# A spectral block on one core: the token table held in full for both halves, fewer filler products, and the special unit two groups later

## The chip, the cores and the metric

The kernel runs on one core of one Trainium2 chip. The metric is device time of one execution in microseconds. Three runs of the kernel as it was before the change gave 255.28 (median), 255.12 and 256.31. A difference of more than 0.5% (about 1.3 us) is about what a measurement of this kernel can tell from no change.

The core has five engines that run their own instruction streams in order: TensorE (PE: matmuls; its weight loads, PEld, overlap the matmuls), VectorE (DVE), ScalarE (ACT), GpSimd (POOL) and SyncE (SP, which issues most DMAs). They wait for one another with semaphores.

## The reference, cut to what matters

```
mod = (silu(c) @ w_mod).reshape(1, 6, 1, 640)      # sa, ca, ga, sb, cb, gb
h = layernorm(x) * (1 + ca) + sa                   # x: 2048 tokens x 640 channels
X = rfft2(h) * (w_r + 1j * w_i)                    # over tokens and channels
x = x + ga * irfft2(X)
h = layernorm(x) * (1 + cb) + sb
x = x + gb * ((silu(h @ w_gate) * (h @ w_up)) @ w_down)   # 640 -> 1728 -> 640
```

All inputs and the output are bf16.

## The kernel before, in words

The work runs in four stages, one after the other.

**The token stage** (lines 326 to 494) normalises x and takes both Fourier transforms as matmuls with tables. A token's number is 1024 h + 8 p + t, with half h = 0 or 1, partition p and residue t = 0 to 7. There is one pass for each residue t:

- `xpair`/`xhat` write the two normalised tiles of the pass (one per half). `rstd_of` takes a short step on VectorE and a power on GpSimd (line 344), then VectorE writes `nmean`, and GpSimd (line 356) or VectorE (line 354) applies them. For passes 4, 5 and 6 GpSimd does both tiles. The tiles lie in three buffers (`xhs`) in turn. The statistics (`bn`, lines 329 and 330) are VectorE's.
- `st_a(t)` (line 370) is ten matmuls. For each of five groups of 128 channels it multiplies half 0's tile and then half 1's tile by 256 columns of the token table `Mtab` (cosines and negative sines of 128 frequencies), and adds the two in PSUM. There is one PSUM area for it, `zA`.
- `ht_ev(t)` (line 373) copies `zA` to bf16 on ScalarE. In pass 7 VectorE copies the last part.
- `st_b(t, ck)` (lines 379 and 381), for ck = 0 and 1, transforms the channels with the tables `Rs`, and `a_ev(t, ck)` (line 385) copies the results into `A_sb`, on ScalarE but for three copies on VectorE and the split last pass.

TensorE's order is `st_a(0)`, then for t = 0 to 7: some filler products (`idle2`, line 362; dummy matmuls into a PSUM bank that nobody reads from there), `st_a(t+1)`, `st_b(t, 0)`, `st_b(t, 1)`. Because `zA` exists once, `st_a(t+1)` may start only when `ht_ev(t)` has read it.

Only half 0's part of the token table is loaded (`load_m`, line 258: 256 columns for each t into the right half of a 512-column row). Moving by 1024 tokens multiplies frequency k by (-1)^k, so half 1's table is half 0's with every second column negated. `m_odd` (line 262, ScalarE, three calls) writes those negated columns into the left half of the row, and half 1's matmuls read columns alternately from the left and the right half:

```
rhs = _rev(Mtab, 512 * t + 256 * (1 - h), [[2, 128], [257, 2]] if h else [[1, 256]])
```

The constants share SyncE's DMA queue with x, the spectral weights and the modulation weights. SyncE issues in program order, and a DMA also waits for the one issued eight before it. GpSimd issues two DMAs (line 282) that write flipped copies of the spectral weights to DRAM; SyncE loads these back later (line 474).

**The mixing stage** (lines 497 to 775) works on 81 channel frequencies l in 21 groups, g = 0 to 20. Each l is a 128x128 block of `A_sb`, which has to be transposed. The first 18 blocks are transposed by TensorE (`t2_pe`); the other 63 by four DMA transposes that SyncE issues as soon as `A_sb` is complete (`t2_dma`, line 509; l = 1 to 15, 16 to 31, 32 to 47, 64 to 79). `mix(g)` (line 547) reads the transposed blocks, `prod` (line 571, VectorE) multiplies by the spectral weights, `stage_b` (line 578) and `stage_c` (lines 600 and 603) transform back, with ScalarE copies (lines 581 and 612) between, into `Em` and `Er`. In the loop over g (line 738), step g does `mix(g+2)`, `prod(g+2)`, `stage_b(g)` and, at every second g, `stage_c`. The first step that reads a block from a DMA transpose is g = 3, with `mix(5)`. GpSimd forms sums of the spectral weights meanwhile (`wsum`, line 390).

**The special unit** is a side computation in this loop for the token frequencies that are multiples of 128; they take partition 127 of `Em` and `Er`. `sp_gather` (line 638, GpSimd) collects one column from all the transposed blocks, so it needs the last DMA transpose. `sp_mm` and `sp_ev` are three rounds of small matmuls and copies, at the steps g in `SPG = (8, 10, 12)`; round 0 (line 647) reads the gathered columns and stands ahead of `mix(g+2)` in TensorE's queue. Round 2 ends with two copies on ScalarE (line 674) and two DMAs that GpSimd issues (lines 675 and 676) into partition 127 of `Em` and `Er`. These have to land before `s1em(0)` (line 697), the first matmuls of the next stage.

**The last two stages** transform back over tokens and channels, add x (lines 1209 to 1266), and run the second layernorm and the feed-forward network (from line 1268), where TensorE is the bound.

The order of the work is written out by hand; no scheduler moves it.

Of the kernel before, what the change touches and what calls it, by code (L numbers as in the profile page):

```python
# [18 lines left out]
NT, P = 16, 128  # L19
# [8 lines left out]
_NPBF = ml_dtypes.bfloat16  # L28
# [59 lines left out]
def _tables():  # L88
    if _TABLE_CACHE:
        return _TABLE_CACHE  # L90
    T = {}
# [8 lines left out]
    p = np.arange(P, dtype=np.float64)  # L100
    kap = p + 1
    M = np.zeros((P, 8, 1, 2, 128))
    H = np.zeros((128, 8, 2, P))
    for t in range(8):
        a = 2.0 * np.pi * ((kap[None, :] * (8 * p[:, None] + t)) % S) / S
        for h in range(1):
            b = 2.0 * np.pi * ((kap[None, :] * (1024 * h + 8 * p[:, None] + t)) % S) / S
            M[:, t, h, 0], M[:, t, h, 1] = np.cos(b), -np.sin(b)
        M[:, t, :, 0, 127], M[:, t, :, 1, 127] = 1.0, ((-1.0) ** p)[:, None]
        H[:, t, 0], H[:, t, 1] = np.cos(a.T), np.sin(a.T)  # L110
        H[127, t, 0], H[127, t, 1] = 1.0, (-1.0) ** p
    T["M"] = M[:, :, 0].reshape(P, 8, 256).astype(_NPBF)
    T["H"] = H.astype(_NPBF)
# [47 lines left out]
def _rev(ap, free_off, dims):  # L161
    a = ap[:]
    return bass.AP(tensor=a.tensor, offset=a.offset + free_off, ap=[list(a.ap[0])] + [list(d) for d in dims])
# [3 lines left out]
def adaln_block_kernel(ctx, tc, A_x, A_w_r, A_w_i, B_x, B_w_gate, B_w_up, B_w_down, c, w_mod, out):  # L167
    nc = tc.nc
    T = _tables()
# [17 lines left out]
    rE = _Region(big, "rE", 40960, "E")  # L187
# [41 lines left out]
    RI = rH.cut(8192, [2, 4, 160])  # L229
    Mtab = rE.cut(0, [8, 512])  # L230
    Rs = rE.cut(8192, [2, 4, RC])
# [25 lines left out]
    def load_m(lo, hi):  # L257
        nc.sync.dma_start(Mtab[:, lo:hi, 256:512], M_dram[:, lo:hi])

    def m_odd(lo, hi):  # L260
        o = Mtab[:, lo:hi].rearrange("p t (b k two) -> p t b k two", b=2, two=2)[:, :, :, :, 0]
        nc.scalar.mul(o[:, :, 0], o[:, :, 1], -1.0)

# [62 lines left out]
    if True:  # L326
# [33 lines left out]
        def idle2(n):  # L360
            for i in range(n):
                nc.tensor.matmul(psum[:, 3, 256:512], lhsT=ones[:], rhs=ones[:].unsqueeze(1).to_broadcast([P, 2, 128]), start=True, stop=True)

        def st_a(t):
            xh = xhs[t % 3]
            for c5 in range(NC5):
                for h in range(2):
                    lhsT = xh[:, h, 512:640] if c5 == 4 else xh[:, h, 0:512].rearrange("p (m r) -> p r m", r=4)[:, c5, :]
                    rhs = _rev(Mtab, 512 * t + 256 * (1 - h), [[2, 128], [257, 2]] if h else [[1, 256]])
                    nc.tensor.matmul(zA[:, c5], lhsT=lhsT, rhs=rhs, start=(h == 0), stop=(h == 1))  # L370

# [41 lines left out]
        nc.scalar.activation(sc_f[:], cps, ACT.Silu)  # L413
        m_odd(0, 1)
        act_stats(3)
# [18 lines left out]
        st_a(0)  # L434
        m_odd(1, 3)
        ht_ev(0)
# [17 lines left out]
        for t in range(8):  # L454
            if t + 1 < 8:
                idle2(6 if t == 0 else 2)
                st_a(t + 1)
                ht_ev(t + 1, 0, 3 if t == 6 else NC5)
                if t == 6:
                    ht_ev(7, 3, 5, nc.vector.tensor_copy)  # L460
            if t == 0:
                m_odd(3, 8)
            u = 2 * t + 6
# [38 lines left out]
    if True:  # L502
# [208 lines left out]
        PPs, Y2s = {}, {}  # L711
        SPG = (8, 10, 12)
        t2_pe(0)
# [24 lines left out]
        for g in range(NG + 1):  # L738
            for lo, rk in {1: ((16, 0), (16, 8)), 4: ((32, 0), (32, 8)), 8: ((64, 0), (64, 8))}.get(g, ()):
                wsum(lo, lo + 16, rk, nc.gpsimd)  # L740
            if g == 3:
                sp_w(1)
            if g == 5:
                nc.gpsimd.tensor_copy(sgnc[:], Kstab[:, 576:577])
            if g == 6:
                sp_gather()
# [620 lines left out]
```

## Time and profile before

| | us |
|---|---|
| three runs | 255.28 median (255.12 to 256.31) |
| the profiled execution | 256.88 |
| its span, from the first to the last instruction | 255.1 |
| busy in the span: TensorE | 245.1 (96%) |
| VectorE | 204.9 (80%) |
| ScalarE | 168.5 (66%) |
| GpSimd | 72.4 (28%) |

The profiled execution took 1.78 us more than its span, and 1.60 us more than the median of the three runs. In the trace the token stage lasts until about 38.6 us of the span, the mixing stage until about 70 us, the stage after it until about 90 us. PE in the profile counts filler products as busy too. "L370" is line 370; "x10" is ten instructions, and the time beside them is that of the group. What stands in square brackets is the engine's idle time before, and who ended it. In the table of windows the columns are the window, its length, the busy time (and number of instructions) of each engine, the granted TensorE clock, the busy share of the DMA engines, and what they moved.

### The profile page before, as it was taken

Reading aid. Unit: us, or ns where it says so; the run is one execution under the profiler, and the core shown is the slowest. Engines: PE = TensorE matmul, PEld = TensorE weight load, DVE = VectorE, ACT = ScalarE, POOL = GpSimd, SP = SyncE. Lnnn points to the kernel's source line nnn. Section 1 sums busy time; section 2 is a strip of 40 time slices with the busy share of each in tenths; the row PEclk is TensorE's granted clock in tenths of the full one; section 3 lists DMA queues with packets and bytes.
Section 4 is the critical chain, followed back from the end, with each engine's and each line's share of the span. In section 5 each row is a group of like instructions: output and inputs, shape, how many; then the busy total and the mean of one; then the engine's idle time right before and its main releaser. Section 6 shows DMA issues by size and latency. Waiting matters only on the chain.

```text
span 255.1 us, 5943 instructions
## 1 busy us (share of the span) xinstructions
PE 245.1 (96%) x2243; PEld 188.4 (74%) x2243; DVE 204.9 (80%) x494; ACT 168.5 (66%) x332; POOL 72.4 (28%) x104
## 2 busy tenths in 40 slices
PE   8799998889989999999999999999999999999994
PEld 3566676889979888778888768888775666556773
DVE  5798359758748999698998996778998788878874
ACT  4786556839789879849876287876336777775220
POOL 5488425574333533200200440000442000003410
PEclk9999999979999999999999999999999999999998
DMA  6999998999976999920000511210511000000111
GB/s 198 331 325 224 333 305 158 178 341 360 250 251 159 271 233 206 184 62 3 1 3 0 103 55 51 30 25 3 104 51 54 0 0 1 3 0 1 54 51 51
DMA packets 42462, 31.99 MB, mean 125 GB/s; under 512 B 21793, under 2 KB 39202, under 8 KB 42434
## 3 DMA queue, kind: packets, MB, share of 16 engines
q1 hardware_dynamic: 40208, 25.97, 38.0%
q0 software_dynamic: 2080, 5.60, 9.9%
q8 instruction: 17, 0.28, 0.5%
q14 instruction: 11, 0.09, 0.1%
q10 hardware_dynamic: 146, 0.04, 0.1%
HBM read 24.28 MB, written 3.94 MB: 111 GB/s over the span
## 4 chain that ended last, share of the span: by engine, by line
PE 87%; ACT 3%; DMA 2%; POOL 2%; issue 2%; DVE 1%; SPq 1%; DVEq 0%; POOLq 0%
PE psum L1088 35%; PE psum L959 18%; PE psum L370 6%; PE psum L1058 6%; PE psum L936 3%; PE psum L697 3%; DMA rE<-tab_M 2%; PE psum L578 2%; PE psum L1229 2%; PE psum L381 2%; PE psum L1232 2%; PE psum L379 2%; PE psum L1046 2%; PE psum L547 2%; PE psum L603 1%
## 5 line engine op out<-in xcount | busy, mean ns | idle before, releaser
L1088 PEld LDWEIGHTS <-rW 128*128 128x128 bf16 (+1 forms) x429 | 42.0, 98 | 12.6
L1088 PE MATMUL psum<-rW 128*128 128x256 bf16 (+1 forms) x247 | 42.2, 287 | 0.0
L985 POOL TENSOR_TENSOR rM<-rM,rL 128x320 f32<-128x320 f32 x6 | 5.4, 905 | 96.6 <-ACT rL L984 96.6
L571 DVE TENSOR_TENSOR rM<-psum,rW 128x384 bf16<-128x384 f32 (+2 forms) x42 | 20.4, 544 | 6.5 <-PE psum L547 5.7
L959 PEld LDWEIGHTS <-rE 128*128 128x128 f16 (+1 forms) x196 | 19.0, 97 | 7.8
L959 PE MATMUL psum<-rE 128*128 128x320 f16 (+1 forms) x147 | 22.9, 299 | 0.0
L1126 ACT COPY rX<-psum 128x384 f32<-128x384 f32 (+2 forms) x27 | 14.0, 519 | 7.5 <-PE psum L1088 7.4
L1088 PEld LDWEIGHTS <-rE 128*128 128x128 f16 x156 | 15.3, 98 | 4.7
L1119 ACT COPY rH<-psum 128x384 f32<-128x384 f32 (+2 forms) x27 | 13.9, 516 | 7.0 <-PE psum L1088 6.3
L1123 DVE TENSOR_TENSOR rH<-psum,rM 128x512 bf16<-128x512 f32 (+1 forms) x24 | 15.0, 624 | 4.1 <-PE psum L1088 2.2
L1142 ACT ACTIVATE rL<-psum 128x384 bf16<-128x384 f32 (+2 forms) x27 | 14.4, 532 | 5.5 <-PE psum L1088 3.4
L370 PE MATMUL psum<-rE 128*128 128x256 bf16 x80 | 16.6, 353 | 1.3 <-DVE rE L354 0.8
L1127 DVE TENSOR_TENSOR rX<-psum,rX 128x384 f32<-128x384 f32 (+2 forms) x27 | 16.3, 605 | 1.6 <-ACT rX L1126 1.4
L1234 DVE SCALAR_TENSOR_TENSOR rM<-psum,rX 128x640 f32<-128x640 f32 x16 | 13.0, 820 | 4.4 <-ACT rL L701 3.2
L1113 ACT COPY rM<-psum 128x384 f32<-128x384 f32 (+2 forms) x27 | 13.9, 515 | 4.0 <-PE psum L1088 3.9
L1088 PE MATMUL psum<-rW,rE 128*128 128x256 bf16 (+1 forms) x78 | 15.6, 290 | 0.0
L1088 PE MATMUL psum<-rE,rY 128*128 128x256 f16 (+1 forms) x78 | 15.6, 290 | 0.0
L581 ACT CAST rY<-psum 128x512 bf16<-128x512 f32 (+2 forms) x21 | 11.8, 583 | 5.5 <-PE psum L578 5.5
L1143 ACT ACTIVATE rL<-rX 128x384 bf16<-128x384 f32 (+2 forms) x27 | 15.1, 558 | 0.0
L370 PEld LDWEIGHTS <-rE 128*128 128x128 bf16 x80 | 8.5, 110 | 8.1 <-issue 6.3
L1058 PE MATMUL psum<-rW 128*128 128x256 bf16 x130 | 14.4, 273 | 0.0
L373 ACT CAST rE<-psum 128x1280 bf16<-128x1280 f32 (+1 forms) x8 | 9.3, 1168 | 7.4 <-PE psum L370 7.4
(232 smaller groups left out, 643.1 us busy)
## 6 DMA issues: line engine op xcount, KB each, us to landing
out_dram<-rA SPq DMA_DIRECT2D x31, 80.0 KB, 1.6
rX<-in_A_x_dram SPq DMA_DIRECT2D x7, 320.0 KB, 6.8
rA<-in_B_w_down_dram SPq DMA_DIRECT2D x2, 960.0 KB, 13.3
rY<-in_B_w_gate_dram POOLq DMA_DIRECT2D x2, 832.0 KB, 6.6
rM<-in_w_mod_dram SPq DMA_DIRECT2D x2, 800.0 KB, 8.8
rM<-in_w_mod_dram SPq DMA_DIRECT2D x1, 1600.0 KB
rW<-in_B_w_gate_dram SPq DMA_DIRECT2D x1, 1440.0 KB, 10.6
rW<-in_B_w_up_dram SPq DMA_DIRECT2D x2, 640.0 KB, 6.7
```

The source lines that it names most:

```text
L370: nc.tensor.matmul(zA[:, c5], lhsT=lhsT, rhs=rhs, start=(h == 0), stop=(h == 1))
L571: nc.vector.tensor_tensor(PPs[g][:, v0:v1, hl], xv[:, v0:v1, hl], in1, ALU.mult)
L959: nc.tensor.matmul(o, lhsT=lhs[rows(k), k], rhs=rhs[rows(k), k], start=start and k == ks[0], stop=stop and k == ks[-1], skip_group_check=True)
L1058: nc.tensor.matmul(gu[u], lhsT=Wgu[:, u, c5, ff * 128:(ff + 1) * 128], rhs=h2T[:, :, c5, :], start=(c5 == 0), stop=(c5 == NC5 - 1))
L1088: nc.tensor.matmul(o[:, f], lhsT=w, rhs=b, start=(start and f == 0 and i == 0), stop=(stop and f == len(groups[g]) - 1 and i == len(ops) - ...
L1113: nc.scalar.copy(c0, X)
L1119: nc.scalar.copy(c2, X)
L1123: nc.vector.tensor_tensor(c11, Z, c0, ALU.add)
L1126: nc.scalar.copy(c3, X)
L1127: nc.vector.tensor_tensor(c22, Y, c3, ALU.add)
L1142: nc.scalar.activation(g21, X, ACT.Silu, scale=-1.0)
L1143: nc.scalar.activation(g22, c22, ACT.Silu, scale=-1.0)
```

## The change

- The host's table gets half 1's columns as well, and the three loads bring both halves: 512 columns for each t instead of 256, contiguous, so 1 MB in place of 512 KB. The memory it lies in is the same.
- The three `m_odd` calls on ScalarE go.
- Half 1's matmuls in `st_a` read 256 contiguous columns.
- One filler product instead of two in passes 1 to 6 (the six ahead of `st_a(1)` stay).
- `SPG` becomes (10, 12, 14): the rounds of the special unit stand two steps later in the loop.
- `sp_gather` is called at g = 8 instead of 6, and the `wsum` of the last 16 frequencies at g = 9 instead of 8. GpSimd's own order changes in one place: the second scaling of `Htab` (line 755) now comes ahead of the special unit's two DMAs instead of after them.

```diff
-    M = np.zeros((P, 8, 1, 2, 128))
+    M = np.zeros((P, 8, 2, 2, 128))
...
-        for h in range(1):
+        for h in range(2):
...
-    T["M"] = M[:, :, 0].reshape(P, 8, 256).astype(_NPBF)
+    T["M"] = M.reshape(P, 8, 2, 256).astype(_NPBF)
...
-    Mtab = rE.cut(0, [8, 512])
+    Mtab = rE.cut(0, [8, 2, 256])
...
-        nc.sync.dma_start(Mtab[:, lo:hi, 256:512], M_dram[:, lo:hi])
-
-    def m_odd(lo, hi):
-        o = Mtab[:, lo:hi].rearrange("p t (b k two) -> p t b k two", b=2, two=2)[:, :, :, :, 0]
-        nc.scalar.mul(o[:, :, 0], o[:, :, 1], -1.0)
+        nc.sync.dma_start(Mtab[:, lo:hi], M_dram[:, lo:hi])
...
-                    rhs = _rev(Mtab, 512 * t + 256 * (1 - h), [[2, 128], [257, 2]] if h else [[1, 256]])
-                    nc.tensor.matmul(zA[:, c5], lhsT=lhsT, rhs=rhs, start=(h == 0), stop=(h == 1))
+                    nc.tensor.matmul(zA[:, c5], lhsT=lhsT, rhs=Mtab[:, t, h], start=(h == 0), stop=(h == 1))
...
-        m_odd(0, 1)
...
-        m_odd(1, 3)
...
-                idle2(6 if t == 0 else 2)
+                idle2(6 if t == 0 else 1)
...
-            if t == 0:
-                m_odd(3, 8)
...
-        SPG = (8, 10, 12)
+        SPG = (10, 12, 14)
...
-            for lo, rk in {1: ((16, 0), (16, 8)), 4: ((32, 0), (32, 8)), 8: ((64, 0), (64, 8))}.get(g, ()):
+            for lo, rk in {1: ((16, 0), (16, 8)), 4: ((32, 0), (32, 8)), 9: ((64, 0), (64, 8))}.get(g, ()):
...
-            if g == 6:
+            if g == 8:
                 sp_gather()
```

## The prediction

> **What bounds the kernel now.** I read the chain of work that ended last, then the order of time of one token pass, then who waits in the mixing stage, then the windows. The chain's shares by engine:
>
> ```profile
> PE 87%; ACT 3%; DMA 2%; POOL 2%; issue 2%; DVE 1%; SPq 1%; DVEq 0%; POOLq 0%
> ```
>
> That reads as "TensorE", but the token stage hides a second bound. One pass in order of time:
>
> ```profile
> 21.93 2.06 PE L370 MATMUL psum<-rE 128*128 128x256 bf16 x10
> 24.07 1.23 ACT L373 CAST rE<-psum 128x1280 bf16<-128x1280 f32 x1 [0.99 <-PE psum L370]
> 24.94 0.38 PE L362 MATMUL psum<-ones 128*128 128x256 bf16 x2
> 25.35 2.05 PE L370 MATMUL psum<-rE 128*128 128x256 bf16 x10
> ```
>
> The next `st_a` starts at 25.35, 0.05 after the copy of `zA` ends (24.07 + 1.23 = 25.30). The loop `st_a`, copy, `st_a` takes 3.42 (25.35 - 21.93); the fillers only fill the wait. So the fillers cost nothing, and a shorter `st_a` is worth its full length, until another loop takes over. That other loop is GpSimd's:
>
> ```profile
> 13.94 0.99 POOL L356 TENSOR_SCALAR rE<-rX,rstd,nmean 128x640 bf16<-128x640 bf16 x1 [0.36 <-DVE nmean L347]
> 17.55 0.87 POOL L356 TENSOR_SCALAR rE<-rX,rstd,nmean 128x640 bf16<-128x640 bf16 x1
> 19.67 1.74 POOL L356 TENSOR_SCALAR rE<-rX,rstd,nmean 128x640 bf16<-128x640 bf16 x2 [0.43 <-issue]
> 22.42 1.73 POOL L356 TENSOR_SCALAR rE<-rX,rstd,nmean 128x640 bf16<-128x640 bf16 x2 [0.36 <-issue]
> 25.16 1.73 POOL L356 TENSOR_SCALAR rE<-rX,rstd,nmean 128x640 bf16<-128x640 bf16 x2 [0.36 <-PE psum L381]
> ```
>
> The pairs for passes 4, 5 and 6 start 2.74 apart, back to back with the power of the next pair. In the mixing stage, the special unit:
>
> ```profile
> 46.65 2.97 SPq L509 DMA_TRANSPOSE rM<-rA  x1
> 51.18 0.97 POOL L638 TENSOR_TENSOR rE<-rM,SA 128x16 bf16<-128x16 bf16 x6 [1.31 <-DMA rM<-rA]
> 52.21 0.31 PE L647 MATMUL psum<-rE 128*81 128x64 bf16 x3 [1.84 <-POOL rE L638]
> ```
>
> The last DMA transpose lands at 51.1, the gather ends at 52.15, and TensorE has stood for 1.84. The windows show what that does to the clock (PEclk, after the five engines), and what the DMA engines moved in two stretches:
>
> ```profile
> 4.60:8.01 3.41, 2.60 (x17) 1.45 (x16) 2.96 (x14) 2.21 (x5) 0.72 (x1) 1.00 1.04 349
> 30.00:31.00 1.00, 1.00 (x9) 0.61 (x8) 0.00 (x0) 0.09 (x1) 0.63 (x1) 1.00 0.99 401
> 36.00:37.00 1.00, 1.00 (x16) 0.84 (x14) 0.76 (x4) 0.26 (x2) 0.57 (x3) 1.00 1.04 284
> 48.97:52.39 3.42, 1.58 (x26) 1.39 (x24) 2.27 (x5) 1.90 (x3) 2.11 (x12) 1.00 0.90 181
> 52.39:55.80 3.41, 3.41 (x32) 3.34 (x31) 1.56 (x6) 1.38 (x2) 3.41 (x5) 0.50 1.01 398
> ```
>
> PE busy 1.58 of 3.42 (46%) was followed by 3.41 us at half clock; 2.60 of 3.41 (76%) was not.
>
> **`st_a` with contiguous columns.** Ten matmuls start within 1.63 (21.9 to 23.5 in the line's answer): five of half 0 and four of half 1 apart. Equal-sized fillers start 0.11 apart (nine in 1.15, the last 0.27 long: 0.88 / 8). So half 1's take (1.63 - 5 x 0.11) / 4 = 0.27, and contiguous ones should take 0.11: 5 x 0.16 = 0.80 off each `st_a`. The loop becomes 2.62, GpSimd's stays at 2.74.
>
> **Table loads and `m_odd`.** 512 KB more in a queue that is saturated to about 37 us. Pieces of 512 bytes came at 284 GB/s (36 to 37, mostly the H table, whose pieces are as long as the old table's), 5 KB rows at 401 (30 to 31, the flipped weights). 512 KB at 284 is 1.85; 1 MB in longer rows at 401 is 2.62: +0.77 for all that follows in the queue, and about +0.34 for what follows the first two table loads (192 of the 512 KB, in the shorter rows). The ends are 0.3 (rows so much better that most is won back) and 1.85 (no better). `m_odd` held ScalarE 0.35 + 0.49 + 0.93; the second one waited for its DMA until 10.16 and held up the first copy of `zA`. Without it that copy ends near 10.5 instead of 11.72, but `st_a(1)` still has the modulation products (25, to 10.35) and six fillers ahead: 11.40 instead of 11.76.
>
> The Trainium skill, page "DMA: Bandwidth & Descriptors", section Specifications, puts line rate at 512 bytes and more, which would make the second half cost its full bytes, an estimated 1.2 to 1.5 us at its 358 to 435 GB/s, against my 0.77; the two rows above disagree with it, 284 against 401 GB/s at a full queue.
>
> **The token stage, walked.** The R table lands at 10.76 and is then 0.34 later, so VectorE's `Rs` (10.86) start at 11.10: +0.24 on the chain to the pair for pass 2 and all of GpSimd's later pairs. Starts of `st_a`, before and after (the later of GpSimd's pair and the 2.62 loop):
> pass 2: 15.13, 15.2 (pair ends 14.93 + 0.24); pass 3: 18.49, 18.7 (pair 18.42 + 0.24, behind the second flip's 1.33 on GpSimd); pass 4: 21.93, 21.7 (pair 21.41 + 0.24); pass 5: 25.35, 24.45 (pair); pass 6: 28.77, 27.2 (pair); pass 7: 32.19, 29.82 (loop; its tile, behind one VectorE copy of pass 4, would be there at 29.1).
> Gain 2.37, and 0.80 in `st_a(7)` itself: **-3.15** at the end of the stage (`A_sb` complete at 35.5 instead of 38.6). Ends: -3.6 (no DMA shift) and -1.6 (one window at half clock inside the stage, 1.5 as priced below).
>
> The queue's landings, from issue, that the next steps use:
>
> ```profile
> rH<-tab_H SPq DMA_DIRECT2D x1, 512.0 KB, 9.7
> rM<-rA SPq DMA_TRANSPOSE x1, 4.5
> rE<-rE POOLq DMA_DIRECT2D x1, 16.0 KB, 7.0
> ```
>
> **First DMA transpose.** `mix(5)` comes at 45.68 - 3.15 = 42.55. The transpose landed at 43.1, 4.4 after its issue at 38.68, and the H table ahead of it in the queue at 40.1. Now it is issued at 35.5 with the H table landing up to 0.77 later, at 40.9; the transpose then lands between 42.5 and 43.9 (40.9 + 3.0). Wait +0 to +1.35, taken **+0.7**, the middle, since neither end has a nearer row.
>
> **Special unit two steps later.** GpSimd's queue holds nothing new ahead of the gather, so the gather still ends 1.03 after the last transpose lands. TensorE gets to step 10 at 42.55 + 0.7 + 4.7 (45.68 to 50.37) + 2.1 (two steps of the pace 56.15 to 58.25) = 50.05. The last transpose lands 8.0 after the first: 51.9 at worst, 48.0 if it moves with the stage. Gather done 49.0 to 52.9, a wait of 0 to 2.85; taken +0.9, as the four transposes together were limited by the DMA engines and partly catch up. With the old 1.84 gone: **-0.94**. The last `wsum` (2.65) follows the gather on GpSimd as before, so it ends by 55.6 at the latest, and `prod(17)` at step 15 needs it, at 62.8 before and some 58 now.
>
> **Clock.** From `mix(10)` at 52.35 to `mix(12)` at 56.15 took 3.8, later pairs of steps 2.1 to 2.5: the half-clock window cost about 1.5. A wait of 0.9 leaves some 70% busy. Whether the three timed runs had that window I can't see, and the profiled one is 1.60 over their median; so **-0.75**, between 0 and -1.5.
>
> **Special unit's end.** From round 2 (58.15) to the landing of its DMAs (60.58 + 7.0 = 67.6) is 9.45, to `s1em(0)` (69.86) it was 11.7, and from step 14 (60.76) it is 9.1. So `s1em(0)` would wait **+0.3** (0 to +1.5, the landing being read from one DMA in a full queue). The second Htab scaling (1.12) now stands ahead of these DMAs on GpSimd, but ends before ScalarE's copies that they wait for. The weights that SyncE loads next land by 76.1 and are used at 89.8; they cover a shift of some us.
>
> **Sum:** -3.15 + 0.7 - 0.94 - 0.75 + 0.3 = -3.84. Against the profiled execution 256.88 gives 253.0; against the median 255.28, **251.4**. All best ends give -6.9, all worst +1.4.
>
> **Rivals.**
> (a) *The transposes don't move* (queue-bound): +1.35 at `mix(5)`, 2.2 at the gather, clock window again: -3.15 + 1.35 - 1.84 + 2.2 + 0.3 = -1.1, 254.2. For it: H table landing at 40.1; against: the transposes' rate isn't steady (205 GB/s from 46 to 48, 160 from 48 to 50), so part can be caught up. 0.15.
> (b) *No new waits*: -3.15 - 1.84 - 1.5 + 0.3 = -6.2, 249.1. 0.15.
> (c) *Half clock in the token stage.* With one filler, passes 2 and 3 leave TensorE about 2.3 of work in 3.4 (some 60 to 70%, between the rows of 46 and 76%). Three such windows at about 1.3 each take back 3.9: 255.3. The Trainium skill, page "TensorE: Matmul & The Clock Gate", section "What's actually happening", wants a whole idle window of 3.4 us before the clock falls, by which this rival would be worth nothing; the row of 46% disagrees, the clock fell after 1.84 idle. 0.08.
> (d) *Slower: the special rows land late.* The DMAs at lines 675 and 676 share the engines with the feed-forward weights, which took 9.8 to 14.6 to land there. At 14 instead of 7.0, `s1em(0)` waits 7 more: 258.4. It decides from a landing time of about 11 up. For it: the slack was 2.3 and is gone; against: their own queue, and 7.0 in that same traffic. 0.06.
>
> **Chances.** Forecast (249.9 to 252.9) 0.56, the four rivals 0.44 together. Faster than 254.0: the forecast, (b), nearly half of (a), some of (c): 0.81. Within 0.5%: the rest of (a) and most of (c): 0.12. Slower: 0.07. Range 248.8 to 254.3.
>
> **What would show it.** Half 1's matmuls 0.11 apart; `st_a` starts 2.6 to 2.75 apart from pass 3 on, each just behind GpSimd's pair; transposes issued near 35.5; a wait of PE for the gather under 1.84 and no half-clock window; `s1em(0)` just behind the special DMA's landing. Wrong if half 1's matmuls stay at 0.27, if PEclk falls in the token stage, or if PE's wait only moves to round 0 at step 10.

## The result, and the profile after

| | before | after |
|---|---|---|
| five runs each, us | 255.54 median (255.12 to 256.31) | 253.23 median (252.68 to 253.96) |
| the profiled execution | 256.88 | 253.96 |
| its span | 255.1 | 252.2 |

The ratio is 0.9906, with a 95% interval of 0.9879 to 0.9934: faster, as forecast, but by 2.3 where 3.8 was forecast (251.4). The time lies in the range (248.8 to 254.3), but not in the narrower band that got most of the chances (249.9 to 252.9).

The lines below answer to those of the prediction. In the new kernel the line numbers are smaller: `st_a` is line 365, `ht_ev` 368, the fillers 358, GpSimd's `xhat` 352, the DMA transposes 500, the gather 629, round 0 of the special unit 638, `mix` 538 and `ga_mod`'s products 672.

First, the shares of the chain that ended last:

```profile
PE 77%; DMA 13%; DVE 4%; SPq 2%; issue 2%; ACT 1%; POOL 0%; DVEq 0%; ACTq 0%; POOLq 0%
```

Before, it was PE 87% and DMA 2%. The chain now runs through the DMA queue, which is the first sign of where the gain went.

Next, one pass of the token stage in order of time (start, length, engine, line, operation):

```profile
23.36 1.73 POOL L352 TENSOR_SCALAR rE<-rX,rstd,nmean 128x640 bf16<-128x640 bf16 x2 [0.36 <-issue]
23.66 1.23 ACT L368 CAST rE<-psum 128x1280 bf16<-128x1280 f32 x1 [0.44 <-PE psum L365]
24.53 0.27 PE L358 MATMUL psum<-ones 128*128 128x256 bf16 x1
24.94 1.38 PE L365 MATMUL psum<-rE 128*128 128x256 bf16 x10
...
26.11 1.73 POOL L352 TENSOR_SCALAR rE<-rX,rstd,nmean 128x640 bf16<-128x640 bf16 x2 [0.36 <-issue]
...
27.69 1.38 PE L365 MATMUL psum<-rE 128*128 128x256 bf16 x10
```

`st_a` starts 2.75 apart (24.94, 27.69) where it was 3.42. GpSimd's pairs also start 2.75 apart (23.36, 26.11). `st_a` begins 0.05 behind the copy of `zA` (23.66 + 1.23 = 24.89), before the second tile of its pair is done (25.09), and its half-1 products wait for that tile, which is why it lasts 1.38 here and not 1.25. The pace is GpSimd's, as the prediction said. Over the kernel the 80 products of `st_a` take 275 ns each instead of 353 by their mean.

Then the passes before that, on TensorE:

```profile
15.93 1.28 PE L365 MATMUL psum<-rE 128*128 128x256 bf16 x10 [1.60 <-POOL rE L352]
...
19.42 1.28 PE L365 MATMUL psum<-rE 128*128 128x256 bf16 x10 [0.98 <-POOL rE L352]
```

The prediction had 15.2 and 18.7 here. TensorE waits for GpSimd's pair, and that chain is 0.9 later than before the change, not 0.24. It begins at x, on VectorE:

```profile
7.12 0.89 DVE L325 BATCH_NORM_STATS2 bn6a<-rX 128x6 f32<-128x320 bf16 x2 [1.58 <-DMA rX<-in_A_x_dram]
```

Before, the same instruction was:

```profile
5.74 0.89 DVE L329 BATCH_NORM_STATS2 bn6a<-rX 128x6 f32<-128x320 bf16 x2 [0.20 <-DMA rX<-in_A_x_dram]
```

The doubled first table load stands ahead of x's tile in the queue. TensorE's last product of the token stage ends at 34.71 instead of 37.27: 2.56 earlier. This is what "the stage ends" means from here on.

In the mixing stage, TensorE's waits and SyncE's issues (the time of an issue holds SyncE's own wait in its queue):

```profile
39.28 0.85 PE L672 MATMUL psum<-rM,sc_rep 128*128 128x320 bf16 x5 [0.89 <-DMA rM<-in_w_mod_dram]
...
44.39 0.42 PE L538 MATMUL psum<-Ktab,rL 128*128 128x192 bf16 x3 [0.28 <-DMA rL<-rA]
```

```profile
32.31 0.65 SPq L469 DMA_DIRECT2D rH<-tab_H  x1
36.25 11.38 SPq L500 DMA_TRANSPOSE rL<-rA  x3
47.80 2.90 SPq L500 DMA_TRANSPOSE rM<-rA  x1
```

```profile
52.10 0.97 POOL L629 TENSOR_TENSOR rE<-rM,SA 128x16 bf16<-128x16 bf16 x6 [1.58 <-DMA rM<-rA]
```

The transposes are issued from 36.25 instead of 38.68, and still the last one lands at 52.0 (51.1 before). So the gather ends at 53.08 and round 0 starts at 53.13 after a wait of 1.83, which before the change was 1.84, two steps of the loop earlier.

The last view is the table of windows: two of the clock's windows in the token stage, then the two around the gather.

```profile
4.75:8.16 3.41, 1.81 (x13) 1.07 (x11) 1.72 (x7) 1.00 (x3) 0.72 (x1) 1.00 1.00 348
14.99:18.40 3.41, 2.47 (x23) 2.08 (x23) 3.31 (x12) 1.73 (x3) 2.83 (x3) 1.00 1.17 328
49.13:52.54 3.41, 2.17 (x33) 2.00 (x32) 2.78 (x6) 2.59 (x4) 0.67 (x4) 1.00 0.98 177
52.54:55.96 3.42, 2.83 (x48) 2.83 (x49) 2.16 (x7) 1.66 (x3) 3.42 (x9) 1.00 0.90 329
```

PE is busy 53 to 83% of these windows and the granted clock (first of the last three columns) stays at 1.00. The wait of 1.83 (51.30 to 53.13) lies across the edge at 52.54 and is shared by two windows.

The sum of the prediction, each term against the two profiled executions:

| term | forecast | measured |
|---|---|---|
| token stage | -3.15 | -2.56 (37.27 to 34.71) |
| waits up to `mix(5)` | +0.7 | +1.27 (`mix(5)` 45.68 to 44.39, so 1.29 of the 2.56 is left) |
| wait for the gather | -0.94 | -0.01 (1.84 to 1.83) |
| half-clock window | -0.75 | about -1.5 (the profiled execution of before had it, this one not) |
| special rows | +0.3 | 0 (the first landed at 65.99, `s1em(0)` at 67.02) |
| sum | -3.84 | -2.8; profiled executions -2.92 |

The profiled execution of the changed kernel is the slowest of its five, 0.73 over their median, so the table, if anything, understates what the change won at the median.

### The profile page after: what moved, and what is told of

Its sections match the earlier page's. It is cut to its first block, busy times and chain, and to the rows that moved or that the text cites. A ratio compares the mean times of both kernels' runs of the same rounds, so it can differ in the third digit from the quotient of the medians.

```text
span 252.2 us, 5929 instructions
## 1 busy us (share of the span) xinstructions
PE 237.0 (94%) x2237; PEld 185.8 (74%) x2237; DVE 204.9 (81%) x494; ACT 166.6 (66%) x329; POOL 72.8 (29%) x104
## 3 DMA queue, kind: packets, MB, share of 16 engines
q0 software_dynamic: 2080, 5.60, 10.5%
## 4 chain that ended last, share of the span: by engine, by line
PE 77%; DMA 13%; DVE 4%; SPq 2%; issue 2%; ACT 1%; POOL 0%; DVEq 0%; ACTq 0%; POOLq 0%
PE psum L1079 35%; PE psum L950 19%; PE psum L1049 6%; DMA wflip_r<-in_A_w_r_dram 5%; DMA rM<-in_w_mod_dram 3%; PE psum L927 3%; PE psum L688 3%; DMA rL<-rA 2%; DMA rX<-in_A_x_dram 2%; PE psum L1220 2%; PE psum L1223 2%; PE psum L1037 2%; SPq L500 1%; DVE bn6a L325 1%; PE psum L569 1%
## 5 line engine op out<-in xcount | busy, mean ns | idle before, releaser
L365 PE MATMUL psum<-rE 128*128 128x256 bf16 x80 | 10.7, 275 | 5.3 <-POOL rE L352 2.6
L325 DVE BATCH_NORM_STATS2 bn6a<-rX 128x6 f32<-128x320 bf16 x28 | 12.3, 479 | 3.1 <-DMA rX<-in_A_x_dram 3.1
L919 DVE TENSOR_TENSOR rA<-psum,rM 128x320 bf16<-128x320 f32 (+1 forms) x27 | 12.1, 472 | 2.4 <-PE psum L927 2.3
```

Source lines behind the costliest of these rows:

```text
L325: nc.vector.bn_stats(bn6a[:, ti % 2, k, :], x_sb[:, ti, 320 * k:320 * k + 320])
```

## The experiments

All of them were timed against the kernel before. In each group of four the kernels ran on one chip and shared its times; those of before were 256.57 median (23 runs) in the first group, 256.49 (28) in the second and 255.39 (22) in the third. They move because the kernel before has two groups of times, and the mean granted clock of each execution tells them apart without an exception: 34 executions of 254.80 to 255.86 have 0.997 to 1.000, 39 of 256.15 to 257.38 have 0.991 to 0.993. A ratio against the kernel before therefore also holds the share of its executions that had the lower clock. "At full clock" below means executions at 0.997 or more; the kernel before has a median of 255.1 there, in every group. Landings named below are those of a DMA's last piece in the trace.

The theory from these profiles (the queue theory): SyncE's DMA queue sets when the transposes land, so the table's shorter passes only lead to a longer wait. Its rival: the parts simply add, each worth its own term.

### The special unit alone

The kernel before, with only the last three edits of the change:

```diff
-        SPG = (8, 10, 12)
+        SPG = (10, 12, 14)
...
-            for lo, rk in {1: ((16, 0), (16, 8)), 4: ((32, 0), (32, 8)), 8: ((64, 0), (64, 8))}.get(g, ()):
+            for lo, rk in {1: ((16, 0), (16, 8)), 4: ((32, 0), (32, 8)), 9: ((64, 0), (64, 8))}.get(g, ()):
...
-            if g == 6:
+            if g == 8:
                 sp_gather()
```

> The kernel before with the special unit's part of the change alone (rounds at steps 10, 12, 14, gather and last weight sum called later); token table and fillers as before. Queue theory (the gather is set by the DMA queue, and the gain comes from two more steps done ahead of it): TensorE reaches step 10 near 52.5, the gather ends near 52.15 as before, so the 1.84 us wait and the half-clock window behind it go, 1.8 to 3.3 us faster than before, as fast as the whole change or faster. Stage theory (the gain is the shorter token stage, carried through): within 0.8 us of before, since the wait only moves to another place.

Measured: 254.23 (253.61 to 255.14), ratio 0.9931 (0.9906 to 0.9955). TensorE in order of time:

```profile
52.45 0.61 PE L578 MATMUL psum<-identb,rM 128*128 128x128 bf16 x8
53.01 0.30 PE L647 MATMUL psum<-rE 128*81 128x64 bf16 x3
```

Round 0 comes at 53.01 with no idle time; the gather had ended at 52.96. With the old table, moving the special unit takes its whole wait away, and all twelve executions are at full clock. At full clock the gain is 0.9 (255.1 to 254.2); the rest of the ratio is the lower clock that is gone. The queue theory had this kernel as fast as the whole change or faster, and that it is not (`two_fillers` below, which adds the table, has 253.36 on the same chip).

### The table alone

The changed kernel with the special unit back at steps 8, 10 and 12, the gather at g = 6, and the last `wsum` at g = 8:

```diff
-        SPG = (10, 12, 14)
+        SPG = (8, 10, 12)
...
-            for lo, rk in {1: ((16, 0), (16, 8)), 4: ((32, 0), (32, 8)), 9: ((64, 0), (64, 8))}.get(g, ()):
+            for lo, rk in {1: ((16, 0), (16, 8)), 4: ((32, 0), (32, 8)), 8: ((64, 0), (64, 8))}.get(g, ()):
...
-            if g == 8:
+            if g == 6:
                 sp_gather()
```

> The changed kernel with the special unit back at steps 8, 10 and 12: the table and the fillers alone. Queue theory: the gather still ends near 53.1 (0.9 later than before), TensorE reaches step 8 near 49.1 and waits some 4 us; 0.9 us slower than before, some 256.2 to 256.6, half clock behind the wait. Stage theory: the gain of 1.3 to 2.5 us is there without the special unit's move, 253.0 to 254.2.

Measured: 256.75 (256.04 to 257.51), ratio 1.002 (0.9996 to 1.0044): no gain. The wait, and the two clock windows around it:

```profile
47.63 0.61 PE L569 MATMUL psum<-identb,rM 128*128 128x128 bf16 x8
52.35 0.30 PE L638 MATMUL psum<-rE 128*81 128x64 bf16 x3 [4.12 <-POOL rE L629]
```

```profile
49.73:53.14 3.41, 0.79 (x13) 0.79 (x14) 0.11 (x1) 0.00 (x0) 1.81 (x8) 1.00 0.83 169
53.14:56.55 3.41, 3.41 (x35) 3.33 (x33) 2.32 (x7) 2.02 (x3) 2.87 (x4) 0.50 1.02 402
```

The token stage ends 3.05 earlier than before (34.22), and the wait for the gather grows from 1.84 to 4.12. The gather ends at 52.3, as before. All twelve executions have a granted clock of 0.986 to 0.993. The rival's 253.0 to 254.2 for this kernel is missed by more than 2: the earlier end of the stage turned into a longer wait.

### The H table behind the transposes

The changed kernel; SyncE issues the H table and RI (used late in the mixing stage) after the four transposes instead of before them:

```diff
-                    nc.sync.dma_start(RI[:], RI_dram)
-                    nc.sync.dma_start(Htab.rearrange("p (t h) v k -> p t h (v k)", h=2)[:, :, 0, :], H_dram.rearrange("p t v k -> p t (v k)"))
...
         t2_dma(3)
+        nc.sync.dma_start(Htab.rearrange("p (t h) v k -> p t h (v k)", h=2)[:, :, 0, :], H_dram.rearrange("p t v k -> p t (v k)"))
+        nc.sync.dma_start(RI[:], RI_dram)
```

> The changed kernel with the loads of the H and RI tables issued behind the four DMA transposes instead of ahead of them. Queue theory: the transposes no longer stand behind 832 KB, the last one lands 2 to 3 us earlier than 52.0 and the gather ends near 50; the 1.83 us wait goes, 1.5 to 2.5 us faster than the changed kernel. If the transposes are paced by SyncE's issue or by themselves, whatever is in the queue: within 0.5 us of the changed kernel.

Measured: 252.32 (252.05 to 252.93), ratio 0.9861 (0.9827 to 0.9896). SyncE's issues and TensorE at round 0:

```profile
35.82 8.77 SPq L498 DMA_TRANSPOSE rL<-rA  x3
44.76 2.80 SPq L498 DMA_TRANSPOSE rM<-rA  x1
47.60 0.66 SPq L508 DMA_DIRECT2D rH<-tab_H  x1
```

```profile
50.15 0.30 PE L638 MATMUL psum<-rE 128*81 128x64 bf16 x3 [0.66 <-DVE rM L562]
```

Three transposes take 8.77 of SyncE's time instead of 11.38, the last lands at 49.04 instead of 52.03, and TensorE stands for 0.66 instead of 1.83 (the gather ends at 50.09, just ahead of it; VectorE's release came beside it). The first transpose's issue, which held SyncE for 5.46 with H ahead (36.25 to 41.71, just before H's last piece landed), takes 2.17. All traces agree: from the first issue to the last landing the four transposes take 14.7 to 15.8 in the five kernels with short passes and H ahead, 12.8 to 13.6 in three with H behind and an equally early stage, and 12.4 to 13.1 in the five with long passes. This shows the cause: with short passes, plain loads queued ahead of the transposes hold them. The time gains about 1.0 on the changed kernel (`two_fillers`, the same chip, at full clock: 253.35), less than the 1.5 to 2.5 expected. The move has a price too, at the modulation products late in the loop:

```profile
58.70 0.40 PE L551 MATMUL psum<-sc_col,rM 128*128 128x1 bf16 x10 [1.31 <-DMA rM<-in_w_mod_dram]
```

Their weights now stand behind H and RI in the queue.

### The first table load behind x

The changed kernel with the t = 0 row of the table loaded after x's tiles 2 to 5:

```diff
-    load_m(0, 1)
     load_x(1)
     load_x(2)
+    load_m(0, 1)
```

> The changed kernel with the first table load (t = 0) issued behind the x tiles 2 to 5 instead of ahead of them. In the changed kernel x tiles 2 and 3 landed at 7.10 (5.72 before) and st_a(0) started at 8.62 (7.24 before). If the doubled first table load is what held x up: tiles 2 and 3 land near 5.5, GpSimd's pairs come 0.7 to 1.0 us earlier and the token stage ends that much earlier. Queue theory: the time stays within 0.5 us of the changed kernel all the same, as the transposes and the gather don't move. Stage theory: 0.7 to 1.0 us faster.

Measured: 252.89 (251.8 to 254.77), ratio 0.9885 (0.984 to 0.993). The first of these tiles landed at 6.13 instead of 7.10, and `st_a(2)` started at 15.39 instead of 15.93. But this landing also moves from run to run: in the kernels that left the doubled load where it was it came at 6.4 to 7.1. The gain of 0.3 in the median lies within the spread of the runs; whether the order of these loads is worth anything can't be told.

### Both queue moves

The edits of the last two sections together.

> The changed kernel with both queue moves at once: the H table and RI issued behind the four transposes, and the table's first row issued behind x's tiles 2 to 5. If each takes its own wait away (the gather's, and x's arrival), they add: st_a starts some 0.3 earlier than with the H move alone, round 0 waits under 0.7, and the time is about 252.0. Rival: what the early loads give is lost again at the next wait in the same queue (the transposes still land by the queue's pace), so the time is that of the H move alone, 252.3, or that of either within its interval, and the gather's wait grows by what the stage gains.

Measured: 252.56 (251.79 to 254.19), ratio 0.9859 (0.9821 to 0.9897): no better than the H move alone, so the rival's time holds. Its reason can't be read here, since in the profiled execution, the slowest of the seven at 254.19, the stage ended late (37.07) for a cause that neither theory had. VectorE in order of time:

```profile
24.40 0.89 DVE L325 BATCH_NORM_STATS2 bn6a<-rX 128x6 f32<-128x320 bf16 x2 [2.88 <-DMA rX<-in_A_x_dram]
```

x's last two loads landed at 24.4 and 24.7, six after the one ahead of them (18.05), beside the flipped weights that GpSimd writes from 10.5 on (that write landed at 24.4 too). TensorE then waited 2.07 and 0.55 in pass 5. Over the traces, x's last load landed between 15.7 and 18.4 in the six kernels with 512 KB of table loaded and between 17.9 and 24.7 in the eight with 1 MB. So it looks as if the doubled table pushes x's tail into this traffic; in the other traces no such wait of TensorE came of it.

### The read alone

The changed kernel with the full load, no negated copies and one filler, but half 1 read as before the change. The host puts half 1's columns first:

```diff
-    T["M"] = M.reshape(P, 8, 2, 256).astype(_NPBF)
+    T["M"] = M[:, :, ::-1].reshape(P, 8, 2, 256).astype(_NPBF)
...
-                    nc.tensor.matmul(zA[:, c5], lhsT=lhsT, rhs=Mtab[:, t, h], start=(h == 0), stop=(h == 1))
+                    nc.tensor.matmul(zA[:, c5], lhsT=lhsT, rhs=_rev(Mtab, 512 * t, [[2, 128], [257, 2]]) if h else Mtab[:, t, 1], start=(h == 0), stop=(h == 1))
```

> The changed kernel with its full table load, without the negated-column copies on ScalarE and with one filler, but half 1's matmuls read their columns alternately from two places 257 apart, as before the change. If the read alone made the passes long, half 1's matmuls go back to 0.27 apart, st_a to 2.06, the passes from 4 on to 3.4, the end of the token stage from 34.7 to about 37.9, and the time to about that of the special unit's move alone, 254.2 to 255. Rival: the passes got short because ScalarE lost the copies (the copy of zA comes sooner); then the starts of st_a stay 2.75 apart and the time stays at 253.2.

Measured: 254.86 (254.24 to 256.04), ratio 0.9959 (0.9934 to 0.9984). The group of `st_a`:

```profile
L365 PE MATMUL psum<-rE 128*128 128x256 bf16 x80 | 16.7, 353 | 1.5 <-POOL rE L352 0.6 <-DVE rE L350 0.2
```

The mean is 353 ns again, `st_a` starts 3.42 apart, and the stage ends at 38.04. The read alone made the passes long; ScalarE's copies and the fillers had no part in it.

### Two fillers

The changed kernel with the second filler back in passes 1 to 6:

```diff
-                idle2(6 if t == 0 else 1)
+                idle2(6 if t == 0 else 2)
```

> The changed kernel with two filler products instead of one ahead of the passes 2 to 7. If TensorE waits there for GpSimd's pair or for the copy of zA anyway, as the trace of the changed kernel shows (0.98 and 1.60 idle ahead of passes 3 and 2), the second filler costs nothing: 253.2, within 0.3. Rival: from pass 4 on nothing is idle any more and each extra filler (0.11 to 0.2) is paid in four or five passes: up to 0.8 later at the end of the stage, of which the transposes' queue would hide a part: 253.3 to 253.8.

Measured: 253.36 (252.73 to 255.15), ratio 0.9902 (0.9874 to 0.9929). That is the time of the changed kernel (253.23); the stage ended at 34.27. The filler costs nothing that these times can tell. Three of the twelve executions have the lower clock (0.992 or 0.993, 253.89 to 255.15); the nine at full clock have a median of 253.35.

### The old table with the H move

The kernel before, with the special unit moved and H and RI behind the transposes, by the edits shown above for each.

> The kernel before, with the special unit moved as in the change, and the H table and RI issued behind the four transposes; the old table, its copies on ScalarE and two fillers stay. If the queue is what keeps the table's gain in the token stage from the end, then here, where the old token stage ends 3 later and TensorE waited for no transpose any more, the H move brings nothing: 254.2, as with the special unit's move alone, and the table is worth about 1.9 once the queue is relieved (254.2 against 252.3). Rival: the H move is worth the same 0.9 whatever the table, by fewer loads beside the transposes: 253.3.

Measured: 255.16 (254.54 to 255.76), ratio 0.9963 (0.9937 to 0.9989). The H move brings nothing here; it costs some 0.9 against the special unit's move alone (254.23), as TensorE had no wait for a transpose to lose and still gets the 1.3 for the modulation weights, seen in the list of waits (engine, line, releaser, total, times, longest):

```profile
PE psum L560 <- DMA rM<-in_w_mod_dram: 1.3, 1, 1.3
```

So what the table is worth depends on the queue. With H ahead of the transposes it adds little to the special unit's move (0.9931 to 0.9906, intervals that overlap); with H behind them it is worth 1% (0.9963 to 0.9861, intervals apart): 2.8 by the medians, where 1.9 was expected.

### TensorE kept busy through the wait

The kernel before, with dummy products ahead of round 0:

```diff
+                if g == 8:
+                    for i in range(24):
+                        nc.tensor.matmul(psum[:, 3, 448:512], lhsT=ones[:], rhs=ones[:, 0:64], start=True, stop=True)
                 if g in SPG:
                     sp_mm(SPG.index(g), g)
```

> The kernel before with 24 dummy products of 64 columns (some 1.2 to 1.4 in all, less than the 1.84 that TensorE stands there) ahead of round 0 at step 8, so that TensorE is busy while it waits for the gather. The times of the kernel before fall in two groups, 254.9 to 255.4 and 256.4 to 257.4, some 1.7 apart. If that is the half-clock window after the wait (it costs about 1.5, and comes or not by where the wait falls in windows that run on their own), then here no window falls to half clock after the gather and only the lower group is left: median 255.1, nothing over 255.8. Rival: the groups come from the order in which the DMAs are served; then both groups stay, median 255 to 256.8.

Measured: 256.16 (255.46 to 256.85), ratio 1.0017 (0.9998 to 1.0036). The windows at the gather:

```profile
48.64:52.06 3.42, 2.76 (x54) 2.49 (x50) 2.78 (x6) 2.41 (x4) 1.74 (x8) 1.00 0.92 142
52.06:55.47 3.41, 2.68 (x45) 2.68 (x46) 2.00 (x7) 1.56 (x3) 3.41 (x10) 1.00 0.96 367
```

The clock stayed full, as expected: the mean granted clock is 0.997 to 1.000 in all twelve executions, while 9 of the 22 of the kernel before beside them had 0.992 or 0.993. One window of 3.41 at half clock takes 0.7% off the mean of a span of 255, which is the step between the two groups above. So the upper group is the executions in which such a window came, and not another order of the DMAs. The expectation of the time is missed: the twelve lie at 256.2, not at 255.1. Of this 1.1, some 0.9 is inside the span (median 254.15, against 253.3 at full clock in the kernel before). The profiled execution is an odd one, with 2.85 between span and time where the other eleven have 1.7 to 2.1. Its trace shows that the products took less than expected and that TensorE still stood for 1.39 after them:

```profile
50.54 0.86 PE L750 MATMUL psum<-ones 128*128 128x64 bf16 x24
52.79 0.31 PE L647 MATMUL psum<-rE 128*81 128x64 bf16 x3 [1.39 <-POOL rE L638]
```

Where the 0.9 arises stays open, since no execution of the kernel before at full clock was traced.

### The columns in another order

The bytes without the slow read: the table's columns that change sign in half 1 stand together, only half 0's 256 are loaded, and ScalarE writes 128 negated columns for each t.

```diff
-    T["M"] = M.reshape(P, 8, 2, 256).astype(_NPBF)
+    T["M"] = M[:, :, 0].reshape(P, 8, 2, 64, 2).transpose(0, 1, 4, 2, 3).reshape(P, 8, 256).astype(_NPBF)
...
-        nc.sync.dma_start(Mtab[:, lo:hi], M_dram[:, lo:hi])
+        nc.sync.dma_start(Mtab[:, lo:hi, 128:384], M_dram[:, lo:hi])
+
+    def m_neg(lo, hi):
+        nc.scalar.mul(Mtab[:, lo:hi, 0:128], Mtab[:, lo:hi, 128:256], -1.0)
...
+                    rhs = _rev(Mtab, 512 * t, [[256, 2], [1, 128]]) if h else Mtab[:, t, 128:384]
...
-            (eng or nc.scalar.copy)(HTs[t % 3][:, lo:hi], zA[:, lo:hi])
+            (eng or nc.scalar.copy)(HTs[t % 3][:, lo:hi].rearrange("p c (k two) -> p c two k", two=2), zA[:, lo:hi].rearrange("p c (two k) -> p c two k", two=2))
```

> The changed kernel, but the table's columns are ordered so that the 128 that change sign in half 1 stand together: only half 0's 256 columns are loaded (512 KB, as before the change), ScalarE writes 128 negated columns for each t beside them, half 1's products read two runs of 128, and the copy of zA puts the columns back in order. If the extra 512 KB in the queue costs what the trace suggests (loads 0.4 to 1.2 later, and x's last tiles pushed into the flipped copies' traffic), then st_a stays at about 0.11 apart and 1.25 long, x's last tile lands by 16.5 as with the old table, the stage ends 0.4 to 0.9 earlier than 34.3 to 34.7, and the time is 252.4 to 252.9. Rival: the bytes don't matter, since the queue's later loads and the transposes set the end: 253.2. If runs of 128 are read as slowly as single columns, 255 to 256.

Measured: 253.38 (251.9 to 254.85), ratio 0.991 (0.9882 to 0.9938): within the noise the time of the changed kernel. Four of the eleven executions had the lower clock; the seven at full clock have a median of 253.0, beside 253.35 in `two_fillers`. The groups of `st_a` and of the copy of `zA` up to 40 us:

```profile
L368 PE MATMUL psum<-rE 128*128 128x256 bf16 x80 | 10.5, 274 | 5.1 <-ACT rE L371 2.0 <-POOL rE L355 1.2 <-ACT rA L383 1.0
```

```profile
L371 ACT CAST rE<-psum 128x1280 bf16<-128x1280 f32 (+1 forms) x8 | 12.2, 1521 | 3.6 <-PE psum L368 3.6
```

Two runs of 128 are read at full speed (274 ns) and x's last load lands at 15.8. But the copy, which now writes every second element, takes 1.59 instead of 1.23, so the loop over `zA` is 2.98 long and takes back what the earlier start won: the stage ends at 34.75. This run doesn't isolate the bytes, as its expectation had it.

### H behind the modulation weights too

The changed kernel with H and RI issued after the first modulation load that follows the transposes, and GpSimd's scalings of H at steps 15 and 16:

```diff
         nc.sync.dma_start(wm_r[:, :, 1:3, :], wm_m[:, :, 1:3, :])
+        nc.sync.dma_start(Htab.rearrange("p (t h) v k -> p t h (v k)", h=2)[:, :, 0, :], H_dram.rearrange("p t v k -> p t (v k)"))
+        nc.sync.dma_start(RI[:], RI_dram)
...
-            if g in (11, 12):
+            if g in (15, 16):
```

> The changed kernel with the H table and RI issued behind the four transposes and also behind the first of the two modulation weight loads that follow them, and GpSimd's two scalings of the H table at steps 15 and 16 instead of 11 and 12. With H right behind the transposes (252.3) TensorE waited 1.3 for these modulation weights. If that is the price of the move, the wait goes and the time is 251.0 to 251.4. Rival: the next thing in the queue takes its place (the special rows or the second modulation load land later than they are needed): 252.3.

Measured: 252.09 (251.47 to 252.69), ratio 0.9862 (0.9831 to 0.9893). The wait of 1.3 is gone from the trace and `s1em(0)` comes at 64.57 instead of 65.53. In the times the gain can't be told from the H move of `h_behind` (252.32). The forecast of 251.0 to 251.4 is missed. The time is the rival's, but not its reason: no new wait of TensorE of that size appears in the stage.

### Ordered columns and the H move together

The edits of the last two sections.

> Ordered columns and the H table behind the modulation load together. If the bytes ahead of the transposes and the bytes beside them are two separate prices, both gains add: 250.3 to 250.9, and the gather has no wait or one under 0.3. Rival: once the transposes land early enough TensorE is never idle there, so that the second gain has nothing to take: equal to the better of the two alone.

Measured: 251.2 (250.61 to 251.7), ratio 0.9824 (0.9793 to 0.9854), the fastest kernel of the study. TensorE at round 0:

```profile
49.60 0.61 PE L576 MATMUL psum<-identb,rM 128*128 128x128 bf16 x8
50.23 0.30 PE L645 MATMUL psum<-rE 128*81 128x64 bf16 x3
```

The last transpose lands at 49.12, the gather ends at 50.17, and TensorE stands for 0.02. Beside the kernel of the last section, on the same chip (252.09), it gains 0.9, though the token stage ends no earlier (34.66 against 34.59). The trace shows half of it at the gather, which ends 0.45 earlier, as the last transpose does; the rest was not located. Its forecast was 250.3 to 250.9, with no wait at the gather: the wait is as forecast, the time is 0.3 over.

## Why the prediction was right, and where it was wrong

The direction was right and the time came into the range, but part of that is luck. The token stage, the wait up to `mix(5)` and the wait for the gather together gave 2.1 less than forecast; the clock and the special rows gave 1.05 more. Of this, 0.75 is there because the profiled execution before happened to have a half-clock window, and the one after had none.

**The shorter `st_a`, and the loop that takes over: right.** The contiguous read took 0.8 off `st_a`, and from pass 4 on GpSimd's 2.75 is the pace. `strided_read` shows that the read was the cause: it alone moves the end of the stage by 3.3, against the 3.15 forecast (by the prediction's own figures 2.37 + 0.80 = 3.17).

**Fillers at no cost: right**, by `two_fillers`.

**Rival (c), half clock in the token stage: wrong.** Windows with PE busy for 53% and 72% of their length, shown above, kept the full clock.

**The early DMAs (+0.24 on GpSimd's chain): wrong, it was +0.9.** The step took only the R table's landing. The second x tile, behind the first table load, landed at 7.10 instead of 5.72 and was last. Part of it is variation: the other kernels with this load in its place and the contiguous read had that tile at 6.4 to 6.8 and ended the stage at 34.2 to 34.6, a gain of 2.7 to 3.1.

**The queue (+0.77): 2.0 in this pair, about 1 over all traces.** The H table, for which the sum used the term, landed at 42.13 instead of 40.09. But this pair is an extreme one. Where the H table stands ahead of the transposes, it landed at 40.0 to 41.3 in the four kernels with 512 KB of table and at 40.6 to 42.3 in the five with 1 MB (means 40.6 and 41.5, so +0.9). `Ktab`, a load ahead of it in the queue, landed at means of 31.2 in six kernels with 512 KB and 32.3 in eight with 1 MB (+1.0). The second flipped copy shows more (34.5 and 36.1, +1.5), but not the queue alone: in every trace SyncE issues its load 0.01 to 0.02 after GpSimd's write of that copy has landed, and with the change GpSimd issues that write later (17.11, not 16.16). The Trainium skill, page "DMA: Bandwidth & Descriptors", section Specifications, with line rate from 512 bytes on, had an estimated 1.2 to 1.5 for the second half of the table. The +0.9 and +1.0 lie between that and the 0.77, and the runs don't decide between the two. (By the step's own rates, 284 and 401 GB/s, its +0.34 for the first two table loads comes to 0.29.)

**The wait up to `mix(5)` (+0.7): 1.27.** Of it 0.28 is the transpose named, and 0.89 a load that the step did not name: `ga_mod`'s modulation weights in the same queue, for which TensorE had no wait before.

**The wait for the gather (+0.9): 1.83, the step that failed most.** "The four transposes together were limited by the DMA engines and partly catch up": they did not. From the first issue to the last landing they took 15.8 instead of 12.4. What held them stood ahead of them: H and RI. This is nearly rival (a), whose price of 2.2 was for a queue that doesn't move at all. With H and RI out of their way (`h_behind`) they take 13.2 and the wait is 0.66, below the forecast. The prediction had a sign for this, "if PE's wait only moves to round 0 at step 10", and it came: 1.84 at step 8 became 1.83 at step 10.

**The clock (-0.75): about right as a mean, but taken from the wrong time.** 39 of the 73 executions of the kernel before had the lower clock, and the medians of its two groups are 1.4 to 1.8 apart, so the mean cost is about 0.85 (an estimate, 39 / 73 of 1.6). But the sum was taken from 255.28, a time of the lower group, where there is no such window to lose. At full clock the change won 1.9 (255.1 to 253.2). All twelve executions of the table alone, whose wait is 4.12, had the lower clock; none of the twelve of the special unit alone, which has no wait, had it. Profiled executions with nearly the same wait fell on both sides, as the windows lay; here PE's busy time (first number after the length) and the next window, for `m0_after_x` (wait 1.83) and then for `ordered_columns` (wait 2.00):

```profile
49.48:52.90 3.42, 1.59 (x28) 1.44 (x26) 1.54 (x4) 1.18 (x3) 2.38 (x9) 1.00 0.82 201
52.90:56.31 3.41, 3.41 (x60) 3.33 (x57) 3.35 (x10) 2.54 (x7) 3.41 (x4) 1.00 1.04 403
```

```profile
49.50:52.91 3.41, 1.42 (x23) 1.26 (x21) 1.42 (x3) 1.56 (x3) 1.65 (x8) 1.00 1.01 212
52.91:56.33 3.42, 3.42 (x36) 3.36 (x34) 2.44 (x7) 1.80 (x3) 3.42 (x5) 0.50 1.03 404
```

46% busy in 3.42 and the clock stays; 42% and it falls. Since the wait of the changed kernel is still 1.83, it keeps this risk: its own five executions are all at 1.00, but three of the twelve with two fillers are not.

**The special rows (+0.3): no wait.** The first, which `s1em(0)` reads, landed in 6.1, not 7.0, and TensorE came later than forecast. The slack is 1.03 where it was 2.26. Rival (d) has no support.

Of what the change won, about three quarters is the special unit's move by the ratios (0.9931 alone, 0.9906 with the table). At full clock it is half: 255.1 before, 254.2 with the special unit moved, 253.35 with the table too (`two_fillers`); the rest of the special unit's part is the half-clock windows that it ends. The forecast had the table as the larger part. It named the queue as a rival, but took the price of the first transpose from a landing of H that came 1.2 earlier than measured (40.9, 42.13), and let the later ones catch up. Its bounds were also added wrongly: all worst ends give +2.3 (-1.6 + 1.35 + 1.01 + 0 + 1.5), not +1.4.

## What to carry to other kernels

When a stage that feeds a DMA gets shorter, read what is queued ahead of that DMA before the gain is counted: a wait behind a full queue moves with the queue and not with the issue. Loads that are needed late belong behind the transfers that the next stage waits for, but also behind nothing that is needed sooner than they are. And a gain that is swallowed is not lost: the same table edit was worth little behind the old queue and 1% behind the reordered one. Where times fall in two groups, compare the groups by their granted clock before comparing medians.

## What the runs showed that was not expected

- **A wait of TensorE of 1.8 to 2.0 costs either its own length or about 1.5 more.** A window of 3.41 with TensorE busy for 46% kept the clock in `m0_after_x`, while the kernel before shows a rounded 46% with a fall; 42% and 23% fell too. The Trainium skill, page "TensorE: Matmul & The Clock Gate", section "What's actually happening", has windows of 3413 ns that run on their own; the edges here agree (47.79, fourteen times 3.41, between two changes of the clock in the kernel before). That page lets the clock fall after a whole idle window; the falls above, after windows that were 23 to 46% busy, disagree.
- **The tail of the H load moves little, with transposes behind it or not.** These are windows of the changed kernel with the queue still full, then while the last of H lands (until 42.1) with the first transpose behind it, then with transposes alone; the last column is GB/s.

```profile
36.00:37.00 1.00, 0.69 (x8) 0.47 (x9) 0.59 (x3) 0.56 (x2) 0.00 (x0) 1.00 1.07 374
40.00:41.00 1.00, 0.82 (x8) 0.59 (x7) 1.00 (x4) 0.42 (x1) 1.00 (x2) 1.00 0.89 45
41.00:42.00 1.00, 1.00 (x17) 0.90 (x16) 0.97 (x4) 0.48 (x2) 0.71 (x2) 1.00 0.19 43
44.00:46.00 2.00, 1.72 (x29) 1.63 (x28) 0.82 (x2) 1.27 (x5) 1.36 (x3) 1.00 1.08 221
```

  From 40 to 42 only some 44 GB/s move, with the DMA engines busy at first (0.89) and then mostly not (0.19). In the kernel before the same stretch came ahead of the transposes, of which the first was issued at 38.68:

```profile
38.00:39.00 1.00, 0.69 (x9) 0.29 (x6) 1.00 (x5) 0.84 (x2) 0.92 (x3) 1.00 0.09 25
39.00:40.00 1.00, 0.92 (x14) 0.92 (x15) 1.00 (x4) 0.34 (x2) 1.00 (x3) 1.00 0.09 24
```

  So the transposes don't cause it; with the earlier stage they stand behind it. Why it is slow is open.
- **The order of elements costs differently by engine.** A moving operand that alternates between two places costs 0.16 more for 256 columns; two runs of 128 cost nothing; a ScalarE copy of 128x1280 from PSUM that writes every second element takes 1.59 instead of 1.23.
- **Products added inside a wait kept the clock full and still cost about 0.9 inside the span** (`kept_busy`). The cause is open.
